# A gated recurrence with a max of three products: another order of all engines' work in the first three steps

## The chip, the cores and the metric

The kernel runs on one core of a Trainium2 chip. The metric is device microseconds of one execution. Executions of one kernel mostly lie within one to two per cent of each other; a run is called slow when it is over 1.5% above the fastest of its kernel, and only fast runs are compared. Where a ratio stands below, it is the mean time of one kernel's fast runs over the mean of the kernel before's fast runs of the same rounds, with a 95% interval, so it is not quite the ratio of the medians that stand beside it. "Faster" and "slower" are said from 2% on.

## The reference, cut to what matters

```python
def _attn_ref(q, k, v, alpha):                 # 4 batches, 8 heads, 768 tokens, 48 wide
    for t in range(S):
        state = alpha[:, :, t, :, None] * state + einsum('bhd,bhe->bhde', k[:, :, t], v[:, :, t])
        y[:, :, t] = einsum('bhd,bhde->bhe', q[:, :, t], state)

def _moe_ref(x, w1, w2, w3, w_out):            # x 3072 x 384, w1..w3 384 x 768, w_out 768 x 384
    h = np.maximum(np.maximum(x @ w1, x @ w2), x @ w3)
    return h @ w_out
```

The output of the first, heads side by side, is x of the second. Inputs and output are float32; the kernel computes in fp16 with float32 sums.

## The kernel before

The tokens are cut into 12 steps of 256 (three chunks of each of four batches). In a step VectorE, GpSimd and ScalarE make scaled forms of q and k; TensorE transposes them (in the later steps the DMA engines do), multiplies them to scores (A), applies the masked scores to the values (Y, attend), updates the state (S), then runs nine groups of gate matmuls (G) with maxima behind them, and two projections (O). The whole program is one list of named pieces per engine order. A piece is a letter, a number, an optional engine or bank letter, and the step after "@".

```python
    pieces = {
        "l": load_step, "K": lambda _, i, *x: load_weight(i), "W": cast_weight, "H": warm,
        "m": pair_decay, "N": logs, "r": inverse, "u": near_k, "w": near_q,
        "c": sums, "e": decay_in, "f": decay_out, "g": totals,
        "k": scale_k, "q": scale_q, "V": values,
        "T": turn, "t": keep_turned, "D": turn_by_dma, "A": scores, "a": masked,
        "Y": attend, "x": keep_x, "M": gates, "S": update, "s": add_state, "z": decay_state,
        "G": gate, "h": maxed, "O": project, "o": store,
    }
    # ...
    with tc.manual_schedule():
        nc.vector.memset(blank, 0.0)
        clear_padding()
        emit(0, PROLOGUE)                      # steps 0, 1, 2 and the start of 3 and 4
        for s in range(3, NS):
            emit(s, LAST if s == NS - 1 else STEADY)
```

Each engine works through its own pieces in the order in which the list names them. A scaled product has two inputs in SBUF and may be given to VectorE ("v") or GpSimd ("p"):

```python
    def scaled(eng, s, r, i, n):
        dst = qks[s % NQ][:, r, i]
        engines[eng or "p"].tensor_mul(
            dst.rearrange("p a b c -> p (a b) c")[:, :, :D],
            near_of.pop((s, n)) if r == 0 else raw(n, s, 1), dec_of[s, n])
```

A gate group is twelve instructions of TensorE, six weight loads and six matmuls of 256 columns:

```python
        for j in range(2):
            jj = 2 * jg + j
            for f in range(NF):                # NF = 3
                nc.tensor.matmul(gps[:, j, :], wcat[:, f, g, jj * P:(jj + 1) * P],
                                 xT[:, f].rearrange("p u t -> p (u t)"),
                                 start=(f == 0), stop=(f == NF - 1))
```

Warm-up: matmuls of 512 columns on zeros whose result nobody reads (53 in the profiled run of the kernel before, 14.9 us busy).

```python
    def warm(_, n, *x):
        wps = bank([P, 512], "wps", "g")
        for _ in range(n):
            nc.tensor.matmul(wps, blank[:, :P], blank, start=True, stop=True)
```

## Time and profile before

| | kernel before |
|---|---|
| time, median of the 3 runs | 157.74 us (156.53 to 159.45) |
| span of the profiled run | 155.9 us |
| first gate matmul | 26.16 us |
| score matmuls of step 4 | 62.08 us |
| distance from one steady step to the next | 10.66 us |
| TensorE at half clock | 19.46 to 22.87 us, and after the end |

TensorE is busy everywhere but at the start, in the fifth slice (15.6 to 19.5 us), and at the end.

### The profile page before, as it was taken

The numbers are of one execution on the slowest core, as the hardware profiler recorded it, in microseconds if no ns is written. First come the engines' busy times: TensorE is split into PE (matmuls) and PEld (weight loads), VectorE is DVE, ScalarE is ACT, GpSimd is POOL, SyncE is SP. The second block draws the span as 40 slices with busy tenths as digits, with TensorE's granted clock in tenths as the row PEclk, the third lists the DMA queues.
The fourth block names the chain that finished last, engine by engine and source line by source line (L and its number), as shares of the span: only waits on it lengthen the run. The fifth ranks groups of instructions, "written<-read, shape, count | busy, mean of one in ns | idle before, by whom it ended". The sixth has DMA issues, their size and how long they took to land.

```text
span 155.9 us, 5905 instructions
## 1 busy us (share of the span) xinstructions
PE 147.8 (95%) x2537; PEld 110.3 (71%) x2537; DVE 127.8 (82%) x210; ACT 77.3 (50%) x152; POOL 88.4 (57%) x128
## 2 busy tenths in 40 slices
PE   6999399999999989999999999999999999999990
PEld 2446177788787778687787786886877877868860
DVE  2239989999876998979989989989898898996560
ACT  3449359475778569165274362471643622023311
POOL 5146970932567908857967967687679674020000
PEclk9999959999999999999999999999999999999999
DMA  5999999999999997099999996989914909411013
GB/s 125 322 325 325 369 349 340 291 298 326 265 280 281 310 289 219 9 166 270 244 162 293 190 231 193 254 225 328 214 50 62 178 4 104 136 50 55 4 70 132
DMA packets 72889, 32.49 MB, mean 208 GB/s; under 512 B 65440, under 2 KB 72864, under 8 KB 72864
## 3 DMA queue, kind: packets, MB, share of 16 engines
q1 hardware_dynamic: 72576, 31.99, 82.6%
q8 instruction: 20, 0.33, 0.9%
q10 hardware_dynamic: 288, 0.13, 0.5%
q14 instruction: 5, 0.04, 0.1%
HBM read 23.73 MB, written 4.72 MB: 182 GB/s over the span
## 4 chain that ended last, share of the span: by engine, by line
PE 84%; DVE 6%; SPq 3%; DMA 3%; issue 1%; ACT 0%; DVEq 0%; ACTq 0%
PE gps L396 46%; PE ops L420 16%; PE yps L330 5%; PE aps L280 5%; PE yps L311 4%; PE sps L368 3%; SPq L95 3%; DMA ra<-in_alpha_dram 3%; PE tps L259 3%; DVE qk L235 1%; PE lps L209 1%; DVE vt L158 1%; PE wps L433 1%; DVE ka L199 1%; DVE pa L184 1%
## 5 line engine op out<-in xcount | busy, mean ns | idle before, releaser
L396 PE MATMUL gps<-xT,wcat 128*128 128x256 f16 x648 | 76.9, 273 | 0.7 <-DVE hT L411 0.7
L396 PEld LDWEIGHTS <-wcat 128*128 128x128 f16 x648 | 61.6, 98 | 10.0 <-issue 0.7
L287 DVE TENSOR_TENSOR lat<-aps,cp 128x512 f16<-128x512 f32 x48 | 30.1, 677 | 0.7 <-PE aps L280 0.7
L383 POOL TENSOR_TENSOR st<-full,gm 128x384 f16<-128x384 f32 x19 | 15.9, 839 | 21.4 <-DVE full L379 13.9
L411 DVE TENSOR_TENSOR h<-gps,h 128x512 f16<-128x512 f32 x36 | 24.4, 683 | 3.5 <-PE gps L396 1.6
L411 DVE TENSOR_TENSOR hT<-gps,h 128x512 f16<-128x512 f32 x36 | 24.5, 689 | 3.2 <-PE gps L396 0.9
L420 PE MATMUL ops<-wo,hT 128*128 128x384 f16 x144 | 27.1, 327 | 0.0
L156 ACT ACTIVATE ob<-ops,c 128x384 f32<-128x384 f32 x23 | 13.4, 583 | 18.7 <-PE ops L420 18.7
L420 PEld LDWEIGHTS <-hT 128*128 128x128 f16 x144 | 13.3, 98 | 7.5
L150 ACT CAST xT<-yps 128x384 f16<-128x384 f32 x14 | 6.5, 479 | 23.3 <-PE yps L330 23.3
L152 DVE CAST h<-gps 128x512 f16<-128x512 f32 x21 | 14.4, 690 | 2.1 <-PE gps L396 2.1
L150 ACT CAST h<-gps 128x512 f16<-128x512 f32 x15 | 8.8, 586 | 14.8 <-PE gps L396 14.7
L433 PE MATMUL wps<-blank 128*128 128x512 f16 x53 | 14.9, 435 | 1.2 <-DVE blank L506 1.2
L203 POOL TENSOR_TENSOR qa<-rq,ra 128x384 f32<-128x384 f32 x10 | 10.0, 1001 | 7.0 <-DMA rq<-in_q_dram 4.5
L353 POOL TENSOR_TENSOR gt<-ge 128x4 f32<-128x4 f32 x18 | 4.0, 220 | 13.9 <-ACT ge L229 13.9
L235 POOL TENSOR_TENSOR qk<-ka,ic 128x384 f16<-128x384 f32 x10 | 10.3, 1028 | 1.6 <-ACT ic L217 1.6
L199 POOL TENSOR_TENSOR ka<-rk,ra 128x384 f32<-128x384 f32 x10 | 10.3, 1033 | 1.4 <-DVE qk L235 1.4
L433 PEld LDWEIGHTS <-blank 128*128 128x128 f16 x53 | 5.4, 110 | 7.9 <-issue 3.3
L330 PE MATMUL yps<-lat,vt 64*32 64x128 f16 x768 | 10.9, 220 | 0.0
L235 POOL TENSOR_TENSOR qk<-qa,ac 128x384 f16<-128x384 f32 x9 | 9.1, 1010 | 2.1 <-ACT ac L223 2.0
L156 ACT ACTIVATE vt<-rv,c 128x768 f16<-128x768 f32 x11 | 10.2, 930 | 0.0
L150 ACT COPY qkT<-tps 128x1024 f16<-128x1024 f16 x7 | 7.0, 1009 | 5.3 <-PE tps L259 5.2
(53 smaller groups left out, 181.1 us busy)
## 6 DMA issues: line engine op xcount, KB each, us to landing
ra<-in_alpha_dram SPq DMA_DIRECT2D x12, 384.0 KB, 5.2
rk<-in_k_dram SPq DMA_DIRECT2D x12, 384.0 KB, 5.3
rq<-in_q_dram SPq DMA_DIRECT2D x12, 384.0 KB, 5.1
rv<-in_v_dram SPq DMA_DIRECT2D x12, 384.0 KB, 5.0
out_dram<-ob SPq DMA_DIRECT2D x24, 192.0 KB, 3.4
ws<-in_moe_w_dram SPq DMA_DIRECT2D x9, 384.0 KB, 7.0
ws<-in_moe_w_out_dram SPq DMA_DIRECT2D x3, 384.0 KB, 6.3
qkT<-qk SPq DMA_TRANSPOSE x14, 4.5
```

What stands on the lines that cost most here:

```text
L150: nc.scalar.copy(out=dst, in_=src)
L152: engines[eng].tensor_copy(out=dst, in_=src)
L156: nc.scalar.mul(dst, src, col)
L199: engines[eng or "p"].tensor_mul(near_of[s, "k"], raw("k", s, 0), raw("a", s, 1))
L235: engines[eng or "p"].tensor_mul(dst.rearrange("p a b c -> p (a b) c")[:, :, :D], near_of.pop((s, n)) if r == 0 else raw(n, s, 1), dec_of[ ...
L287: nc.vector.tensor_mul(lat_of[s, u][:, i].rearrange("p (a r) t -> p a r t", r=R), aps_of[s, u][i].rearrange("p (a r) t -> p a r t", r=R), ...
L330: nc.tensor.matmul(yps[x][C * m:C * (m + 1), f, :], vt[rows, r * HP + p].rearrange("p a b -> p (a b)")[:, at:at + C], lats[p // (HP // R)] ...
L383: engines[eng or "p"].tensor_mul(sts[s % B][1 - x].rearrange("p a (b d) -> p a b d", d=D), full_of.pop((s, x)), gm_of.pop((s, x)).unsqueez ...
L396: nc.tensor.matmul(gps[:, j, :], wcat[:, f, g, jj * P:(jj + 1) * P], xT[:, f].rearrange("p u t -> p (u t)"), start=(f == 0), stop=(f == NF ...
L411: nc.vector.tensor_max(h, gps, h_of[s, i - 1])
L420: nc.tensor.matmul(ops, hT_of[s][:, jj, u * P:(u + 1) * P], wo16[:, jj, :], start=(jj == 0), stop=(jj == NJ - 1))
L433: nc.tensor.matmul(wps, blank[:, :P], blank, start=True, stop=True)
```

## The change

The intent is to order the work of all engines in the first three steps afresh, so that fewer of VectorE's SBUF products run at the same time as GpSimd's. No arithmetic changes. The diff replaces the three strings of pieces; their first lines and one steady step:

```diff
     PROLOGUE = """
-        m0v@0 r0@0 r1@0 H2@0 H1@0 H4@0 H2@0 H2@0 H3@0 l0@1 w0p@0 u0v@0
-        H2@0 l0@2 l1@2 l1@1 N0@0 l2@1 c0@0 l2@2 l3@1 K4@0 H2@0 e0@0
-        H2@0 m0v@1 H1@0 N0@1 H2@0 H2@0 f0@0 m0v@2 H3@0 H4@0 r0@2 K3@0
-        g0@0 r0@1 V0v@0 N0@2 H3@0 k1p@0 K0@0 H1@0 H2@0 c0@1 e0@1 q1v@0
(4 lines cut)
-        A0g@0 a3@0 a0@0 a2@0 a1@0 l3@3 l1@4 l2@4 T1g@2 t0a@1 H3@0 l0@5
-        r1@2 H2@0 M0p@0 z0p@0 t1a@2 s1@0 w0v@2 l3@4 A1@1 a2@1 V0@1 W4p@0
-        Y0g@0 x0v@0 W3a@0 x1@0 W0p@0 W1a@0 q0v@2 M0p@1 A0g@1 S0@1 s0a@1 a0@1
-        z0p@1 W2a@0 W5p@0 a3@1 G0@0 l3@5 T0@2 G1@0 a1@1 G3@0 l1@5 W7p@0
-        W6a@0 h0v@0 G4@0 h3@0 G2@0 W8p@0 s1a@1 m0p@3 Y0@1 t0@2 x1@1 h1@0
+        r0@0 l0@1 H8@0 m0v@0 l0@2 r1@0 H3@0 N0@0 l1@1 H2@0 c0g@0 H1@0
+        l2@1 w0v@0 e0@0 k1p@0 f0@0 l3@1 l2@2 l1@2 q0p@0 g0@0 H3@0 H2@0
+        H1@0 l3@2 H2@0 q1v@0 H3@0 H3@0 l0@3 u0v@0 M0v@0 H2@0 k0v@0 m0v@2
+        l0@4 V0@0 T0@0 T1@0 t0@0 m0p@1 r0@1 K0@0 K1@0 r1@1 K3@0 K2@0
(4 lines cut)
+        T1g@1 T0g@1 H2@0 V0@1 q0v@2 t1a@1 t0@1 u0v@2 S0@1 A0g@1 V0@2 k1p@2
+        s0a@1 l1@5 M0v@1 A1@1 a0@1 q1p@2 Y0g@0 r0@3 l1@4 a2@1 k0p@2 T1g@2
+        a1@1 x0@0 l0@5 t1a@2 l3@6 l2@6 z0p@1 a3@1 T0@2 Y0g@1 t0@2 x1@0
+        A1g@2 A0@2 m0p@3 m0p@4 s1@1 x0@1 l3@4 W0v@0 a2@2 l2@5 x1@1 M0v@2
+        W1a@0 N0@4 S0@2 W3p@0 W2p@0 G0@0 s0@2 a3@2 W5p@0 G0@1 a1@2 W4p@0
(the rest of both PROLOGUEs cut)
     STEADY = """
-        T0@1 G0@0 N0@2 t0a@1 c0@2 g0@2 f0@2 G3@0 u0p@2 T1@1 G4@0 h0v@0
-        e0@2 M1p@-2 z1p@-2 h3v@0 G5@0 r0@3 r1@3 h4@0 G1@0 G6@0 h5@0 h1@0
-        t1a@1 M0p@1 k0p@2 S0@1 k1v@2 w0p@2 V0@2 s0@1 z0p@1 A0g@1 q1p@2 D1@2
+        w0v@2 T1g@1 N0@2 t1@1 M0p@1 u0p@2 T0@1 G0@0 G3@0 h3@0 c0@2 G4@0
+        g0@2 e0@2 t0a@1 h0v@0 G5@0 G1@0 V0@2 f0@2 h4@0 h5@0 h1@0 M1p@-2
+        k0v@2 z1p@-2 G6@0 S0@1 A0g@1 k1p@2 s0@1 h6@0 A1@1 O1g@-1 O0@-1 z0p@1
(the rest of STEADY, and LAST, cut)
```

In the old order the first gate (G0@0) stands between the attends of steps 0 and 1 (Y0g@0, Y0@1). In the new one both attends, the remaining transposes and the scores of step 2 come before it.

More of the change, by code (lines that the diff above doesn't have):

```diff
@@ L463 @@
     PROLOGUE = """
-        m0v@0 r0@0 r1@0 H2@0 H1@0 H4@0 H2@0 H2@0 H3@0 l0@1 w0p@0 u0v@0
-        H2@0 l0@2 l1@2 l1@1 N0@0 l2@1 c0@0 l2@2 l3@1 K4@0 H2@0 e0@0
-        H2@0 m0v@1 H1@0 N0@1 H2@0 H2@0 f0@0 m0v@2 H3@0 H4@0 r0@2 K3@0
-        g0@0 r0@1 V0v@0 N0@2 H3@0 k1p@0 K0@0 H1@0 H2@0 c0@1 e0@1 q1v@0
-        H2@0 K1@0 k0v@0 K2@0 K6@0 K5@0 r1@1 l3@2 c0g@2 H2@0 K7@0 S0@0
-        g0@2 k1v@1 K8@0 u0v@2 M0v@2 q0p@0 l0@3 w0v@1 l0@4 g0@1 l2@3 f0@1
-        T0@0 e0@2 q1v@1 T1@0 K11@0 f0@2 k0v@2 q0v@1 t0a@0 H3@0 H3@0 u0p@1
@@ L471 @@
-        l1@3 t1a@0 T1g@1 s0a@0 K9@0 K10@0 A1@0 k1p@2 k0p@1 t1@1 T0g@1 q1p@2
-        A0g@0 a3@0 a0@0 a2@0 a1@0 l3@3 l1@4 l2@4 T1g@2 t0a@1 H3@0 l0@5
-        r1@2 H2@0 M0p@0 z0p@0 t1a@2 s1@0 w0v@2 l3@4 A1@1 a2@1 V0@1 W4p@0
-        Y0g@0 x0v@0 W3a@0 x1@0 W0p@0 W1a@0 q0v@2 M0p@1 A0g@1 S0@1 s0a@1 a0@1
-        z0p@1 W2a@0 W5p@0 a3@1 G0@0 l3@5 T0@2 G1@0 a1@1 G3@0 l1@5 W7p@0
-        W6a@0 h0v@0 G4@0 h3@0 G2@0 W8p@0 s1a@1 m0p@3 Y0@1 t0@2 x1@1 h1@0
-        h4@0 h2@0 A0g@2 a0@2 x0@1 a1@2 A1@2 G6@0 h6v@0 V0@2 G5@0 h5@0
@@ L478 @@
-        S0@2 s0a@2 l0@6 r0@3 l1@6 m0p@4 G0@1 h0v@1 a2@2 G1@1 l3@6 r1@3
-        N0@3 G7@0 G3@1 l2@6 h1@1 h7@0 G8@0 G6@1 l2@5 h3@1 h6@1 h8@0
-        a3@2 G2@1 z0v@2 c0@3 h2@1 g0@3 r0@4 w0p@3 G4@1 Y0g@2 N0@4 G7@1
-        f0@3 M0p@3 x1@2 u0p@3 x0@2 h4@1 q0v@3 q1v@3 G5@1 e0@3 G0@2 h7@1
-        G8@1 c0@4 h5@1 r1@4 h0@2 G6@2 G1@2 k0p@3 G7@2 h8@1 h6v@2 k1p@3
-        W10a@0 l2@7 G8@2 W11a@0 g0@4 V0@3 h7@2 h1@2 T0g@3 W9p@0 O1@0 T1@3
-        M1v@0 h8@2 f0@4 s1a@2 o1@0 O0g@1 t1a@3 t0@3 u0p@4 e0@4 z1p@0 o0@1
@@ L485 @@
-        G3@2 S0@3 A0g@3 h3@2 l1@7 l0@7 l3@7 s0@3 a1@3 w0p@4 a0@3 q1v@4
-        q0p@4 A1@3 z0p@3 r0@5 O0g@0 a2@3 G2@2 O1@1 a3@3 o0@0 m0v@5 r1@5
-        V0@4 G4@2 Y0g@3 h2@2 k1p@4 h4@2 x0v@3 o1@1 G5@2 h5@2 s1@3 x1@3
-        k0p@4
+        r0@0 l0@1 H8@0 m0v@0 l0@2 r1@0 H3@0 N0@0 l1@1 H2@0 c0g@0 H1@0
+        l2@1 w0v@0 e0@0 k1p@0 f0@0 l3@1 l2@2 l1@2 q0p@0 g0@0 H3@0 H2@0
+        H1@0 l3@2 H2@0 q1v@0 H3@0 H3@0 l0@3 u0v@0 M0v@0 H2@0 k0v@0 m0v@2
+        l0@4 V0@0 T0@0 T1@0 t0@0 m0p@1 r0@1 K0@0 K1@0 r1@1 K3@0 K2@0
@@ new lines @@
+        K5@0 S0@0 K4@0 K6@0 K7@0 K8@0 s0a@0 l1@3 t1@0 H2@0 u0p@1 r0@2
+        l2@3 r1@2 H1@0 A0g@0 A1g@0 N0@1 K9@0 H2@0 K11@0 a2@0 z0p@0 K10@0
+        a0@0 c0@1 e0@1 w0p@1 a1@0 H4@0 g0@1 k0v@1 l2@4 N0@2 a3@0 k1p@1
+        f0@1 c0@2 s1a@0 f0@2 e0@2 q1v@1 l3@3 H3@0 g0@2 w0p@2 H2@0 q0v@1
+        T1g@1 T0g@1 H2@0 V0@1 q0v@2 t1a@1 t0@1 u0v@2 S0@1 A0g@1 V0@2 k1p@2
+        s0a@1 l1@5 M0v@1 A1@1 a0@1 q1p@2 Y0g@0 r0@3 l1@4 a2@1 k0p@2 T1g@2
+        a1@1 x0@0 l0@5 t1a@2 l3@6 l2@6 z0p@1 a3@1 T0@2 Y0g@1 t0@2 x1@0
@@ new lines @@
+        A1g@2 A0@2 m0p@3 m0p@4 s1@1 x0@1 l3@4 W0v@0 a2@2 l2@5 x1@1 M0v@2
+        W1a@0 N0@4 S0@2 W3p@0 W2p@0 G0@0 s0@2 a3@2 W5p@0 G0@1 a1@2 W4p@0
+        W6p@0 h0@0 N0@3 a0@2 G1@1 z0v@2 G1@0 r0@4 h0@1 G3@0 s1a@2 r1@4
+        c0@3 G2@0 Y0@2 h1@1 h1@0 x0@2 h2@0 G2@1 h3v@0 G4@0 h2@1 c0@4
+        G5@0 f0@3 h4@0 G6@1 W7a@0 h5@0 G6@0 r1@3 e0@3 x1v@2 G7@0 W8p@0
+        h6v@0 g0@3 G3@1 M0v@3 h6@1 g0@4 G8@0 G7@1 h7@0 h8@0 G4@1 u0v@3
+        w0p@3 h3@1 G5@1 h7@1 e0@4 G8@1 G0@2 M1p@0 q1v@3 f0@4 z1p@0 W9a@0
@@ L489 @@
+        k0p@3 h4@1 h5@1 h8@1 k1v@3 l1@6 l3@5 G6@2 G8@2 G7@2 h6@2 h7@2
+        h8@2 T1@3 l0@6 q1v@4 h0@2 w0v@4 G3@2 h3@2 G4@2 q0p@3 W10p@0 t1@3
+        T0g@3 W11p@0 O1g@0 O0g@0 V0@3 S0@3 t0@3 h4@2 s0a@3 o1v@0 A1@3 l0@7
+        z0p@3 o0@0 A0g@3 O0g@1 a3@3 a0@3 a1@3 O1@1 G5@2 a2@3 o1v@1 h5@2
+        Y0g@3 m0p@5 r0@5 l1@7 l3@7 o0@1 s1@3 G1@2 r1@5 x1@3 x0@3 G2@2
+        q0p@4 u0p@4 k1p@4 V0@4 k0v@4 l2@7 h1@2 h2@2
     """
     STEADY = """
-        T0@1 G0@0 N0@2 t0a@1 c0@2 g0@2 f0@2 G3@0 u0p@2 T1@1 G4@0 h0v@0
@@ L492 @@
-        e0@2 M1p@-2 z1p@-2 h3v@0 G5@0 r0@3 r1@3 h4@0 G1@0 G6@0 h5@0 h1@0
-        t1a@1 M0p@1 k0p@2 S0@1 k1v@2 w0p@2 V0@2 s0@1 z0p@1 A0g@1 q1p@2 D1@2
-        A1@1 h6@0 a1@1 O0g@-1 G7@0 a0@1 O1@-1 a2@1 a3@1 q0p@2 D0@2 Y0g@1
-        o0@-1 h7@0 s1@1 G8@0 l3@5 x0@1 m0p@3 G2@0 o1@-1 x1v@1 h8@0 h2@0
-        l2@5 l0@5 l1@5
+        w0v@2 T1g@1 N0@2 t1@1 M0p@1 u0p@2 T0@1 G0@0 G3@0 h3@0 c0@2 G4@0
+        g0@2 e0@2 t0a@1 h0v@0 G5@0 G1@0 V0@2 f0@2 h4@0 h5@0 h1@0 M1p@-2
+        k0v@2 z1p@-2 G6@0 S0@1 A0g@1 k1p@2 s0@1 h6@0 A1@1 O1g@-1 O0@-1 z0p@1
@@ L497 @@
+        G7@0 a0@1 a2@1 q0p@2 q1p@2 a1@1 a3@1 D0@2 D1@2 Y0g@1 s1@1 m0v@3
+        h7@0 o1@-1 o0@-1 x0@1 G8@0 x1v@1 h8@0 G2@0 h2@0 l1@5 l3@5 l2@5
+        l0@5 r0@3 r1@3
     """
     LAST = """
-        G0@0 G3@0 G1@0 G2@0 h0v@0 G7@0 h1@0 h2@0 h3@0 G6@0 h6@0 O1@-1
-        G8@0 G4@0 h7@0 h8@0 h4@0 G5@0 o1@-1 O0g@-1 h5@0 O1@0 O0@0 o0@-1
+        G0@0 G7@0 G6@0 h6v@0 O0@-1 G3@0 h0@0 G8@0 h7@0 h3v@0 G1@0 h8@0
+        h1@0 G4@0 G5@0 o0@-1 h4@0 h5@0 G2@0 h2@0 O1g@-1 o1@-1 O1@0 O0@0
         o1v@0 o0@0
```

## The prediction

> **Names.** A piece is a letter, a number and the step after "@": c sums, T transposes, A scores, Y attend, S state update, G one of a step's nine gate groups, O output projection, H n warm-up matmuls of no use, W0 to W11 casts of weights. A last letter v, p or a puts the work on VectorE, GpSimd or ScalarE.
>
> **What bounds the kernel now.** I read the page's first two parts, then the chain that ended last, then the timelines of TensorE, VectorE and GpSimd one after another. From the chain:
>
> ```profile
> 62.08 0.57 PE aps L280 x32
> ...
> 72.75 0.57 PE aps L280 x32
> ...
> 83.42 0.57 PE aps L280 x32
> ...
> 94.08 0.57 PE aps L280 x32
> ```
>
> The columns are start, duration and what. The score matmuls of a steady step return every 10.66 us, and TensorE is busy between them: one step is A 0.57, two O 0.98 + 1.08, Y 1.33, nine G at 0.655 (5.9), S 0.44 and c about 0.3, together 10.6. So steady steps are TensorE's own work; a new order there can lose time, not gain it. VectorE is next: 18.7 us busy in the four stretches from 85 to 105 us, 94%. The only idle times of TensorE over 0.5 us after the first gate are one of 0.67 us ("DVE hT", at 55.7) and small ones of 0.2 to 0.3. What can be won lies before the first gate, and TensorE's timeline shows it:
>
> ```profile
> 7.18 4.91 PE L433 MATMUL wps<-blank 128*128 128x512 f16 x22
> ...
> 14.12 1.07 PE L259 MATMUL tps<-cp,qk 128*128 128x128 f16 x16
> 15.03 1.46 PE L433 MATMUL wps<-blank 128*128 128x512 f16 x6
> 18.89 0.62 PE L259 MATMUL tps<-cp,qk 128*128 128x128 f16 x8 [2.41 <-DVE qk L235]
> ...
> 26.16 0.81 PE L396 MATMUL gps<-xT,wcat 128*128 128x256 f16 x6
> ```
>
> L433 is warm-up, so from 7.2 to 18.9 us TensorE does some 3 us of useful work. At 18.89 it has waited 2.41 us for a product of VectorE; the first gate is at 26.16. The two engines behind that wait, VectorE first:
>
> ```profile
> 13.92 1.35 DVE L199 TENSOR_TENSOR ka<-rk,ra 128x384 f32<-128x384 f32 x1
> 15.19 0.95 DVE L353 TENSOR_TENSOR gt<-ge 128x4 f32<-128x4 f32 x1
> 16.18 0.92 DVE L355 TENSOR_TENSOR gm<-gt,c 128x8 f32<-128x8 f32 x1
> 17.02 0.55 DVE L203 TENSOR_TENSOR qa<-rq,ra 128x384 f32<-128x384 f32 x1
> 17.49 1.34 DVE L235 TENSOR_TENSOR qk<-rq,ac 128x384 f16<-128x384 f32 x1
> ```
>
> ```profile
> 13.61 1.24 POOL L199 TENSOR_TENSOR ka<-rk,ra 128x384 f32<-128x384 f32 x1 [1.43 <-DVE qk L235]
> 14.81 1.31 POOL L235 TENSOR_TENSOR qk<-rk,ic 128x384 f16<-128x384 f32 x1
> 16.09 0.99 POOL L235 TENSOR_TENSOR qk<-ka,ic 128x384 f16<-128x384 f32 x1
> 17.04 1.38 POOL L235 TENSOR_TENSOR qk<-rq,ac 128x384 f16<-128x384 f32 x1
> ```
>
> A VectorE product takes 0.55 us undisturbed (17.02) and 1.35 beside GpSimd; the 4-element gt takes 0.95 where the same operation at 46.6 us took 0.15. They alternate: the VectorE product of 13.92 ends at 15.27, some 0.45 after GpSimd's ended at 14.85, and GpSimd's next, from 14.81, ends 0.85 after that. [...]
>
> [...] 48 masks have a mean of 0.677 us, close to their 0.68 with GpSimd idle. [...] here warm-up matmuls are issued every 0.43 us until 5.4 us, then every 0.21. So 13 of them before c@0 rather than 16 end about 0.5 us earlier.
>
> **The change part by part.** The arithmetic stays: the same pieces, of which some 60 move between VectorE, ScalarE and GpSimd. Although it is named for the first steps, the diff also rewrites the steady and last orders.
>
> *Before the first gate.* Before it, the old order does T@0, T@1, T1@2, A@0, A@1, Y@0, S@0, S@1; the new one also T0@2 (0.45), A@2 (0.57), Y@1 (1.17, from 29.97 to 31.14) and S@2 (0.45). TensorE's total is fixed (warm-ups: 53 to 46), so what counts is the first gate's start less this: break-even is 26.16 + 2.64 = 28.80 us.
>
> *When the new first gate can start.* Its W0 is now VectorE's, after nearly all of two steps' work there. I walk the queues with the measured durations.
> - c@0 at 6.3; its two exponentials end at 7.3 and 7.6. VectorE then has q1, u, M and k0 of step 0 (0.47 each back to back, M 0.3) beside GpSimd's k1, q0 and m@1. Free of collisions, T0@0 starts at 10.0; strictly alternating, at 12.0. It was 14.12.
> - The two transposes (0.9), two copies on VectorE (1.2) and A (0.6 with its latency): masks begin between 12.5 and 15.2, against 20.3.
> - From there to the end of W0 VectorE needs: eight masks 4.8, four products for q and k of steps 1 and 2 1.9, t0@1 and t0@2 1.2, u@2 0.47, M 0.3, s1 twice 1.0, W0 0.5 to 0.8: 10.3 us. Waiting for T0@1 and A@1 adds about 0.6; collisions with GpSimd's k1@1, w@2, k1@2, q1@2, k0@2 add 0 to 2.9.
> - End of W0: best 12.5 + 10.3 + 0.6 = 23.4; worst 15.2 + 10.3 + 0.6 + 2.9 = 29.0. The best is cut by two things. The first weight now comes after 14 loads of steps, not 11; at 1.2 us each and 5 to 7 us to landing it arrives at 22 to 24, and the following, cast by GpSimd, every 1.0 to 1.2 us. ScalarE begins step 1's logarithm only after s0@0, so c@1, at 11.93 before, moves to 13.5 to 15.6. I take 25.3 to 29.0.
>
> The walk's worst case is pessimistic where it lets the engines alternate each time; the intent says that collisions become fewer. I choose 27.2: a gain of 28.8 - 27.2 = 1.6 us.
>
> *From the first gate to step 3.* Old: 26.16 to 62.08, 35.9 us, of which 34.5 is useful work by my addition (27 + 6 gates 21.6, four O 3.9, and 9.0 of T, A, Y, S and c). At most 1.4 can be won. VectorE starts this stretch with eight pieces of step 2 (4.3 us) ahead of its first maximum, but four gate banks and ScalarE's copies cover that. I count 0 for that.
>
> *Steady steps.* VectorE gains w (0.47) and m (0.47) and loses a copy to ScalarE (0.67); its k product, 0.95 now because it collides, may fall to 0.55. From 10.0 of 10.66 it comes to 9.9, or to 11.2 if all three collide at 0.95. TensorE waits only if m, now ahead of the maximum of gate 7, is late: after the last mask come s1 0.5, m 0.5 to 0.9 and the maximum 0.6, 1.6 to 2.0 in all, and the bank is wanted 2.0 after the mask. I allow 0.1 us for each of six steps as a mean of 0 and 0.2: plus 0.5, rounded down as I think 0 likelier. GpSimd falls from about 8.5 to 6.5 us a step, worth nothing.
>
> *End.* Nine gates and four projections remain in both last orders, 5.9 + 3.9 us; 0 within 0.2.
>
> Sum: 157.74 - 1.6 + 0.3 = 156.4; of the 1.4 us of stalls between the first gate and step 3 a better order should find a third, which makes 156.0.
>
> **Rivals.**
> 1. [...] VectorE's products now stand at T0@0 and T0@1 beside GpSimd's own, and more queue ahead of W0 than before. For it: strict alternation in the trace. Against: masks and copies from PSUM lie between them. First gate at 29: 157.9, no change.
> 2. *The collisions go and the weights' landing becomes the bound.* First gate at 25.3, gain 3.5: 154.2. For it: the transfers run at some 325 GB/s without a gap from 5 us on. It needs both engines' queues free of waits.
> 3. *VectorE becomes the steady bound.* It is at 94%; if all its SBUF products collide, a step needs 11.2 us of it and seven steps lose up to 0.5 each: 159 to 160. Against: GpSimd is idle for 4 us of each new step.
>
> **Range and chances.** 2% is 3.15 us, so faster needs nearly all of rival 2, and slower needs rivals 1 and 3 together with more. The three runs of before spread over 2.9 us. I take 153.0 to 158.6, with 0.25 faster, 0.70 within 2%, 0.05 slower.
>
> **What would show it.** Right: T0@0 near 11, first gate near 27 with three S and three A ahead of it, score matmuls of steady steps 10.66 us apart, those at 62.08 now near 60.4, VectorE's k product at 0.55 in steady steps. Wrong: a first gate at 29 with VectorE's products at 0.9 to 1.35 (rival 1), or at 25 (rival 2); a period above 10.7 with "DVE h" waits of TensorE (rival 3); or gates after the first that wait for weights or for VectorE's backlog of step 2.

## More of the kernel before

Attend is 64 small matmuls on tiles of 64 by 32 (and 12 on the state in the first four steps, 24 later), each with a weight load of its own (the page of the changed kernel counts 768 matmuls and 768 loads of this line in 12 steps), so over 150 instructions:

```python
                        nc.tensor.matmul(
                            yps[x][C * m:C * (m + 1), f, :],
                            vt[rows, r * HP + p].rearrange("p a b -> p (a b)")[:, at:at + C],
                            lats[p // (HP // R)][rows, i, p % (HP // R) * R + r, :], ...)
```

From the page of the kernel before: busy time of each engine with its share of the span, then TensorE's busy share and the granted clock in 40 equal slices (9 is 90% or more, 5 is half speed), then the queue that carries instructions (transfers, MB, share).

```profile
PE 147.8 (95%) x2537; PEld 110.3 (71%) x2537; DVE 127.8 (82%) x210; ACT 77.3 (50%) x152; POOL 88.4 (57%) x128
...
PE   6999399999999989999999999999999999999990
...
PEclk9999959999999999999999999999999999999999
...
q8 instruction: 20, 0.33, 0.9%
```

## The result

| | before | changed |
|---|---|---|
| median | 157.13 us (156.47 to 159.45, 4 runs) | 162.65 us (161.96 to 163.71, 4 runs) |
| span of the profiled run | 155.9 us | 160.1 us |
| ratio | | 1.0371 [1.027, 1.0473]: slower |

The four runs of the changed kernel are fast. Of the four of the kernel before, 159.45 us is slow by the rule of 1.5%, and the ratio leaves it out. The time lies 4 us above the predicted range. The page of the changed kernel:

```profile
PE 147.5 (92%) x2530; PEld 109.7 (69%) x2530; DVE 131.8 (82%) x222; ACT 77.2 (48%) x154; POOL 79.9 (50%) x114
...
PE   7978678399999999999999999999999999999990
...
PEclk9999999779999999999999999999999999999999
...
q8 instruction: 20, 0.33, 0.8%
...
L330 PE MATMUL yps<-lat,vt 64*32 64x128 f16 x768 | 11.3, 221 | 2.8 <-issue 2.8
```

GpSimd has indeed lost work (88.4 to 79.9 us). But the eighth slice of TensorE, 28 to 32 us, is only 30% busy, and the clock is reduced there. The last line is attend's group; its final column says that TensorE stood idle for 2.8 us ahead of one of these matmuls, and that nothing in the profile released it: "issue". TensorE's timeline (start, duration, what, count, idle before) shows the place:

```profile
27.51 0.29 PE L330 MATMUL yps<-lat,vt 64*32 64x128 f16 x10
30.57 0.30 PE L330 MATMUL yps<-lat,vt 64*32 64x128 f16 x6 [2.77 <-issue]
30.80 1.07 PE L280 MATMUL aps<-qkT 48*64 48x128 f16 x32
31.80 0.82 PE L368 MATMUL sps<-vt,qk 64*128 64x96 f16 x16
32.55 4.03 PE L396 MATMUL gps<-xT,wcat 128*128 128x256 f16 x30
```

The attend of step 1 stops after 10 of its last 16 matmuls. These 16 use the same values and the same masked scores as the ones before them; no data can be missing for six of them alone. Then all that follows is stretched: the scores take 1.00 us from start to start where they took 0.57, the first gate matmuls 0.21 us each instead of 0.11. The same kinds of work in the kernel before:

```profile
27.26 2.78 PE L396 MATMUL gps<-xT,wcat 128*128 128x256 f16 x24
...
31.14 0.64 PE L280 MATMUL aps<-qkT 48*64 48x128 f16 x32
```

The view of one stretch says why (columns: stretch, its length, busy time of TensorE, weight load, VectorE, ScalarE and GpSimd with counts, granted clock, DMA share, GB/s):

```profile
30.36:33.77 3.41, 3.20 (x60) 2.44 (x60) 2.05 (x6) 2.02 (x4) 1.67 (x3) 0.50 1.07 295
```

The clock is granted at half speed (0.50) for 3.41 us, from 30.36, 0.21 us before TensorE runs again after 2.77 us of idle time.

**Where the 4.2 us of span went.** The standstill is 2.77. The half clock costs 0.43 on the scores (1.00 against 0.57, by starts), 0.30 on the state update (0.75 against 0.45) and 0.58 on the first 30 gate matmuls (3.86 against 3.28 in h1 and c1 below), together 1.31. The sum is 4.08. It is all there by step 4, and little is added after it. From the chain that ended last:

```profile
66.16 0.57 PE aps L280 x32
...
76.83 0.57 PE aps L280 x32
```

Step 4 begins 4.08 us later than before (62.08), and the steady distance is 10.67.

**The kernel before has a half clock too.** Its profiled run has one such stretch (19.46 to 22.87), the changed one has one. The mean granted clock of a run tells how many it had: one stretch of 3.41 us in 156 makes 0.989. Of 39 runs of the kernel before in the rounds of s1, s2, h1 and r1, the five at 0.998 or more took 156.6 to 157.0 us, the 28 at 0.987 to 0.989 took 157.6 to 158.9, the five at 0.978 took 159.0 to 159.3. So one stretch costs it about 1.2 us (an estimate from these runs), and the sum above is not the whole comparison: the half clocks of the two kernels nearly cancel, and beside the standstill some 1.3 us (4.2 - 2.77, less the 0.1 by which 1.31 exceeds 1.2) must come from the new start itself. The experiments h1 and c1 show from where.

**What stopped TensorE.** What I found at the standstill is a transfer of the instruction queue. It makes 20 transfers of 16,384 bytes in either kernel. I counted TensorE's records (matmuls and weight loads each count one). From the start of the first transfer to that of the last TensorE begins 4,829 records in the kernel before (190 to 5,019) and 4,796 in the changed one (221 to 5,017), 254 and 252 from one transfer to the next. In this kernel and in the experiments below, the standstills without a data wait came after record 701, 702, 703 or, in c1, 957, so 254 to 256 apart. From these counts I estimate that TensorE gets its instructions in blocks of about 256, one transfer (a fetch, below) for each, and that a new block begins at about record 191 + 256k; the exact record is an inference, and so is that the transfers are TensorE's. The times in the tables are read from the records and the packets of the trace, as no view prints them. As the fetch of the block from 703 on I take the transfer that starts next after record 447, where by this count the block before it is entered:

| run | enters 447 at | fetch of the next block | enters 703 at | gap there |
|---|---|---|---|---|
| before | 24.70 | 27.36 to 28.43 | 30.33 | none |
| changed | 24.05 | 27.84 to 28.92 | 30.57 | 2.99 |

The gap is from one matmul's start to the next one's, so it is 0.2 us more than the idle time in the timeline. In both kernels the fetch starts 2.7 to 3.8 us after the block was entered and takes 1.1. Resumption follows its end by 1.65. The kernel before needed its new block 1.90 us after the fetch had ended, and so passed with a quarter of a microsecond to spare, if it takes as long to resume. It got through because it spends 5.6 us on the 256 instructions from 447 to 703: 30 gate matmuls of 0.11 us are among them, 24 of them in the line shown above. The changed kernel runs a whole series of small matmuls there, attend, transposes, attend, and was through in 3.5 us. This is theory F (fetch), an inference that the experiments below test. The rival C says that collisions between VectorE and GpSimd, or something else that the new order does to data, delays TensorE (some expectations below call it D or V).

### The profile page after: what moved, and what is told of

It is laid out like the page before. It is cut to its first block, busy times and chain, and to the rows that moved or that the text cites.

```text
span 160.1 us, 5903 instructions
## 1 busy us (share of the span) xinstructions
PE 147.5 (92%) x2530; PEld 109.7 (69%) x2530; DVE 131.8 (82%) x222; ACT 77.2 (48%) x154; POOL 79.9 (50%) x114
## 4 chain that ended last, share of the span: by engine, by line
PE 85%; DVE 8%; issue 4%; ACT 1%; ACTq 0%; DVEq 0%
PE gps L396 44%; PE ops L420 15%; PE yps L330 6%; PE wps L433 4%; PE aps L280 4%; PE yps L311 4%; PE sps L368 3%; PE tps L259 3%; DVE qk L235 3%; DVE ka L199 1%; PE lps L209 1%; DVE lat L287 1%; DVE h L411 1%; DVE gm L355 1%; ACT ic L217 1%
## 5 line engine op out<-in xcount | busy, mean ns | idle before, releaser
L420 PE MATMUL ops<-wo,hT 128*128 128x384 f16 x144 | 25.5, 327 | 0.0
L150 ACT CAST h<-gps 128x512 f16<-128x512 f32 x24 | 14.0, 586 | 23.3 <-PE gps L396 20.6
L156 ACT ACTIVATE ob<-ops,c 128x384 f32<-128x384 f32 x21 | 12.2, 581 | 22.9 <-PE ops L420 22.9
L353 POOL TENSOR_TENSOR gt<-ge 128x4 f32<-128x4 f32 x16 | 5.8, 362 | 19.4 <-ACT ge L229 19.4
L433 PE MATMUL wps<-blank 128*128 128x512 f16 x46 | 13.7, 447 | 2.0 <-DVE blank L505 1.2
L235 POOL TENSOR_TENSOR qk<-rk,ic 128x384 f16<-128x384 f32 x11 | 11.0, 996 | 6.1 <-ACT ic L217 5.0
L330 PEld LDWEIGHTS <-vt 64*32 64x32 f16 x768 | 7.4, 90 | 5.4 <-issue 2.9
L235 POOL TENSOR_TENSOR qk<-qa,ac 128x384 f16<-128x384 f32 x10 | 10.6, 1059 | 0.0
L152 DVE CAST h<-gps 128x512 f16<-128x512 f32 x12 | 8.2, 686 | 1.6 <-PE gps L396 1.6
L259 PE MATMUL tps<-cp,qk 128*128 128x128 f16 x80 | 6.0, 219 | 3.7 <-DVE qk L235 3.4
```

Of the source, the lines that this page charges most:

```text
L150: nc.scalar.copy(out=dst, in_=src)
L156: nc.scalar.mul(dst, src, col)
L235: engines[eng or "p"].tensor_mul(dst.rearrange("p a b c -> p (a b) c")[:, :, :D], near_of.pop((s, n)) if r == 0 else raw(n, s, 1), dec_of[ ...
L259: nc.tensor.transpose(tps[:, i, p, :], qks[s % NQ][:, r, i, p].rearrange("p a b -> p (a b)"), ident)
L330: nc.tensor.matmul(yps[x][C * m:C * (m + 1), f, :], vt[rows, r * HP + p].rearrange("p a b -> p (a b)")[:, at:at + C], lats[p // (HP // R)] ...
L420: nc.tensor.matmul(ops, hT_of[s][:, jj, u * P:(u + 1) * P], wo16[:, jj, :], start=(jj == 0), stop=(jj == NJ - 1))
```

## The experiments

All outputs are right.

### Which string holds the loss

```diff
 s1:  PROLOGUE of the changed kernel
-     STEADY, LAST of the changed kernel
+     STEADY, LAST of the kernel before
```

> The new order of the first three steps with the old steady and last orders. Theory F: TensorE's standstill of 2.8 us inside the attend of step 1 is a wait for its next block of 256 instructions, asked for while the transfers of weights are queued; with the half clock that follows it is nearly the whole loss. So this run keeps it: ratio to before 1.03 to 1.04, a gap of 2 to 3 us at TensorE's instruction 703, first gate at 32 to 33. Rival S, the rewritten steady and last orders cost part of it: ratio below 1.02.

163.41 us median (4 runs), ratio 1.0336 [1.0266, 1.0407].

```diff
 s2:  STEADY, LAST of the changed kernel
-     PROLOGUE of the changed kernel
+     PROLOGUE of the kernel before
```

> The old order of the first three steps with the new steady and last orders. Theory F: no gap, ratio 0.995 to 1.005. Rival S: ratio above 1.015.

157.53 us median (20 runs) against 157.82, ratio 0.9971 [0.9945, 0.9997]. The whole loss is in the first steps; the new steady order even gains 0.3%. That is what the steady VectorE shows. A scaled product of k, first in the kernel before, then in the changed one:

```profile
83.19 0.95 DVE L235 TENSOR_TENSOR qk<-rk,ic 128x384 f16<-128x384 f32 x1
```

```profile
87.18 0.55 DVE L235 TENSOR_TENSOR qk<-ka,ic 128x384 f16<-128x384 f32 x1
90.97 0.55 DVE L184 TENSOR_TENSOR pa<-ra 128x384 f32<-128x384 f32 x1
```

The first (0.95 us) began 0.53 us before the end of a GpSimd product (82.72 to 83.72), the second (0.55) 0.12 us before the end of one (86.30 to 87.30). So the k product no longer collides, and neither does the pair product that VectorE took over (0.55). VectorE's busy time in a steady distance falls from 10.01 to 9.80 us, GpSimd's from 8.17 to 6.65.

### An earlier fetch by quiet data queues

TensorE's fetch takes place while the loads of data run (340 GB/s from 24 to 28 us in the kernel before, 362 in the changed one). Here the loads from the third weight on wait on GpSimd until the time of the fetch, so that the data queues are nearly empty (each load named in the last two lines is taken from its old place):

```diff
+    def hold(_, i, *x):
+        nc.gpsimd.memset(stage[i][:, :1], 0.0)      # piece Q; the load into stage[3] waits for it
 PROLOGUE of the changed kernel:
-    ... K0@0 K1@0 r1@1 K3@0 K2@0 K5@0 S0@0 K4@0 K6@0 K7@0 K8@0 s0a@0 l1@3 t1@0 ...
+    ... K0@0 K1@0 r1@1 S0@0 s0a@0 t1@0 ...
-    ... a2@1 k0p@2 T1g@2 ...
+    ... a2@1 k0p@2 Q3@0 K3@0 K2@0 K5@0 K4@0 K6@0 K7@0 K8@0 l1@3 l2@3 K9@0 K11@0 K10@0
+        l2@4 l3@3 l1@5 l1@4 T1g@2 ...
```

> The changed kernel, with the third weight transfer and all later loads held until GpSimd has finished its product for k of step 2 (a memset of one column of that weight's buffer stands there, so that the transfer has to wait for it, at about 24.7 us). The transfer queues are then nearly empty when TensorE enters its third block of instructions at 24.0 us. Theory F: the fetch starts within 1.2 us of that in place of 3.8, the gap at instruction 703 falls from 3.0 to under 0.6 us, no half clock at 30 us, first gate at 29 to 29.6 (VectorE's cast of the first weight ends at 28.9), ratio 1.00 to 1.015 although the weights land up to 6 us later. Rival D, the gap is a wait for data or buffers: gap unchanged, ratio 1.035 or more.

158.8 us median over 20 runs, ratio 1.0021 [0.999, 1.0051]. This kernel scatters: about 8 of its 20 runs, from 159.4 us up, count as slow and are left out, and only one run was traced, so it is open whether the long ones had a standstill (one of them, 160.18 us, had a mean clock of 1.0, so no half clock made it long). If they had, the hold does not always help, and the ratio of the fast runs holds for the cases where it does; the mean of all 20 is 159.4 us (157.9 before). The traced one (158.51 us, fast) had nearly none. TensorE's timeline at the same place:

```profile
28.13 0.29 PE L330 MATMUL yps<-lat,vt 64*32 64x128 f16 x10
28.60 0.24 PE L330 MATMUL yps<-lat,vt 64*32 64x128 f16 x6 [0.19 <-issue]
...
29.79 3.45 PE L396 MATMUL gps<-xT,wcat 128*128 128x256 f16 x30
```

The stop is after the same ten matmuls, but 0.19 us long. The stretch from 24 to 28 us of the changed kernel, then of this one (columns as above):

```profile
24.00:28.00 4.00, 3.45 (x158) 2.50 (x143) 4.00 (x8) 2.00 (x4) 3.83 (x5) 1.00 1.11 362
```

```profile
24.00:28.00 4.00, 4.00 (x198) 3.15 (x192) 3.96 (x8) 2.76 (x5) 3.67 (x5) 1.00 0.32 96
```

With 96 GB/s of data instead of 362, and none at all from 23.3 us until the fetch, the fetch started 0.83 us after its block was entered (25.16), not 3.79, and ended at 27.25; record 703 was entered at 28.60, 1.35 later. Except for the loads and the hold, order, engines and products are those of the changed kernel. Theory F holds for the standstill. Without it the new order is no slower than the old one in the mean, but its fast runs were at full clock more often: 8 of 12 had a mean clock of 0.996 or more, against 6 of 34 of the kernel before. At like clock h1 is slower: 157.1 to 158.9 us at 0.996 or more (156.6 to 157.7 before), and 158.5 to 159.1 at 0.984 to 0.989 (157.6 to 158.9, median 157.8, before). About 1 us is thus left that is not the standstill.

### Fewer small matmuls before the boundary

```diff
-    ... T0@2 Y0g@1 t0@2 x1@0 A1g@2 A0@2 m0p@3 m0p@4 s1@1 x0@1 l3@4 W0v@0 a2@2 l2@5 x1@1 M0v@2 ...
+    ... T0@2 t0@2 x1@0 A1g@2 A0@2 m0p@3 m0p@4 s1@1 l3@4 W0v@0 a2@2 l2@5 M0v@2 ...
-    ... W2p@0 G0@0 s0@2 ...
+    ... W2p@0 G0@0 Y0g@1 x0@1 x1@1 s0@2 ...
```

> The changed kernel with the attend of step 1 (and its two evictions) moved behind the first gate, so that the scores of step 2, the state update and the first gate come before it. The same instructions; fewer of them stand in a row before the first gate, which waits for VectorE's cast anyway. Theory F: instruction 703 is reached at about 30 us in place of 27.6, the gap there is under 1 us, first gate at 29 to 29.5, ratio 1.00 to 1.02. Rival D: the gap inside the attend stays at 2.5 us or more, ratio 1.03 or more.

161.13 us (4 runs), ratio 1.0214 [1.0163, 1.0265]: some two fifths of the loss are back, slightly less than I had expected. Its timeline:

```profile
31.38 0.50 PE L330 MATMUL yps<-lat,vt 64*32 64x128 f16 x36 [0.35 <-issue]
...
33.32 0.93 PE L396 MATMUL gps<-xT,wcat 128*128 128x256 f16 x7 [0.98 <-ACT xT L150]
```

The stop shrinks from 2.77 to 0.35 us and the clock stays full, as F has it, for now 6.5 us lie between entering the two blocks (24.88 and 31.38). What I had not reckoned with are data waits that the removed attend used to cover: 1.19 us before the scores of step 2 (at 28.48), and 0.98 us of the gate of step 1, whose x is now late.

### Are the collisions enough?

Kernel c1 is h1 with all of step 0's products on VectorE, without any of GpSimd's beside them; c2 is the same with the loads left where the changed kernel has them.

```diff
-    ... H8@0 m0v@0 l0@2 ... w0v@0 e0@0 k1p@0 f0@0 ... q0p@0 g0@0 ... q1v@0 ... u0v@0 M0v@0 H2@0 k0v@0 ...
+    ... H8@0 m0v@0 u0v@0 l0@2 ... e0@0 f0@0 ... g0@0 w0v@0 k1v@0 k0v@0 q1v@0 q0v@0 M0p@0 ...
```

> The changed kernel with the held loads (as h1_quiet), and with all six products of step 0 on VectorE, in an order that uses its idle time (k0 times alpha before q0 lands), step 0's two gate products on GpSimd: no product of step 0 can collide. Prices the collisions of step 0. If they are on the path to the first gate (rival 1 of the prediction): transposes of step 0 finish by 10.5 us (12.7 in the changed kernel), first gate 1.5 to 2.3 us earlier than h1_quiet's 29.8, ratio 0.985 to 0.995. If the later chain (ScalarE's exponentials, landings) decides: first gate within 0.6 us of h1_quiet's, ratio 1.00.

c1: 156.69 us (12 runs), ratio 0.9953 [0.9917, 0.9989], on the edge of what I expected. The transposes of step 0 run in one piece at 10.19 us, where the changed kernel interrupts them by 0.98 us of waiting and begins the second part at 11.89. The first gate starts at 27.50, 2.3 earlier than in h1 (a part of this is a half clock that h1 has from 20.48 to 23.89 and c1 has not). All 12 runs have a mean clock of 0.995 or more; in the same rounds the kernel before took 156.5 to 156.9 us at 0.997 or more. So c1 wins back the 1 us that h1 had lost, and beats the kernel before only in that none of its runs shows a half-clock stretch. The stop moved to the next boundary (after record 957) and is short:

```profile
33.09 0.35 PE L330 MATMUL yps<-lat,vt 64*32 64x128 f16 x20 [0.36 <-issue]
```

> c1_no_collision without the held loads: the changed kernel with step 0's products on VectorE alone. Separates what c1 won by fewer collisions from what it won by quiet queues. Theory F: weights are queued when TensorE asks for its fourth block, so a gap of 1 to 3.5 us at instruction 703 returns, first gate 29 to 31, ratio 1.01 to 1.03. If the collisions alone had been the fault of the changed kernel (rival V): no gap, ratio 0.99 to 1.00 as in c1.

c2: 161.19 us (4 runs), ratio 1.0223 [1.0168, 1.0277]. Its timeline:

```profile
25.90 0.28 PE L330 MATMUL yps<-lat,vt 64*32 64x128 f16 x9
28.58 0.31 PE L330 MATMUL yps<-lat,vt 64*32 64x128 f16 x7 [2.40 <-issue]
```

With the collisions of step 0 gone TensorE arrives at the boundary 1.6 us sooner and stands still there for 2.40 us, again with the half clock after it (28.18 to 35.01). So the collisions of step 0 are not what stops TensorE. They cost those 1.6 us: c1 shows that removing them gains (0.9953 against h1's 1.0021), but only if the instructions come.

### The loss made in the kernel before

If F is right, small matmuls put into the kernel before must bring the standstill there too, although nothing of its data changes.

```diff
+    def crowd(_, n, *x):
+        wps = bank([P, 512], "wps", "g")
+        for _ in range(n):
+            nc.tensor.matmul(wps, blank[:, :P], blank, start=True, stop=True)
+        for i in range(48):                             # 96 in p2
+            m, rows = i % 4, slice(0, J)
+            nc.tensor.matmul(wps[C * m:C * (m + 1), :P],
+                             blank[rows, :C], blank[rows, :P], start=True, stop=True)
 p1, PROLOGUE of the kernel before:
-    ... T1g@2 t0a@1 H3@0 l0@5 ...
+    ... T1g@2 t0a@1 P3@0 l0@5 ...
 p2, PROLOGUE of the kernel before:
-    ... Y0g@0 x0v@0 W3a@0 x1@0 W0p@0 W1a@0 q0v@2 M0p@1 A0g@1 ...
+    ... Y0g@0 x0v@0 W3a@0 x1@0 W0p@0 W1a@0 q0v@2 M0p@1 P0@0 A0g@1 ...
```

> The kernel before, with 48 small matmuls of the attend's shape (no use, into the bank of a warm-up) added to that warm-up at 22.4 us, where TensorE is ahead anyway. Alone they cost about 1 us, partly in a wait. Theory F: they make 96 more instructions, so TensorE enters its next block that much earlier in its work, at about 28.5 us in place of 30.3, while the block lands no earlier than before (the fetch ended at 28.4 and TensorE needs 1.5 us more). So a gap of 1 to 2 us with no releaser appears at instruction 703, among the gates; ratio 1.008 to 1.025. Rival D: no such gap, ratio 1.00 to 1.006.

p1: 158.66 us (17 runs), ratio 1.0057 [1.0027, 1.0087], and no standstill in the traced run. My expectation missed. Its blocks explain how, though not why: the block was entered at 23.93, the fetch ran from 24.92 to 26.04, only 0.99 us later with the loads of the kernel before, where 351 GB/s ran during a lag of 2.66 us, and record 703 was entered at 28.02. The added matmuls ran at 22.26 and moved the boundaries as planned: the block lasted 4.09 us, 5.63 before. What spared it was the early fetch. So the lag between entry and fetch does not seem to be set by the traffic of data alone.

> The kernel before, with 96 small matmuls of the attend's shape (192 instructions, no use) between the attend of step 0 and the scores of step 1, right behind the point at which TensorE enters its third block of instructions (24.7 us in before). In p1_crowd 48 of them took 0.8 us, so these take 1.6 to 2.2. Theory F: the next block is needed 192 instructions earlier in the work, at about 27.5 us, and cannot be there before about 29 (in all runs TensorE entered a block no sooner than 1.3 us after its fetch had ended): a gap of 1 to 3 us with no releaser at instruction 703, which none of the data explains; ratio 1.015 to 1.04. Rival D: no gap beside the added work, ratio 1.008 to 1.015.

p2 puts twice as many into the block itself. 164.63 us (4 runs), ratio 1.0413 [1.0324, 1.0502]. Its timeline:

```profile
25.47 1.52 PE L441 MATMUL wps<-blank 64*32 64x128 f16 x96
26.92 0.30 PE L280 MATMUL aps<-qkT 48*64 48x128 f16 x7
29.92 0.52 PE L280 MATMUL aps<-qkT 48*64 48x128 f16 x9 [2.69 <-issue]
```

1.52 us of work that nobody needs cost 6.3 us (164.63 against 158.31 in the same rounds). TensorE stops within the scores, after record 702, for 2.69 us, and the half clock follows (29.68 to 33.09). The order of all other work, and its collisions, are those of the kernel before. The standstill is therefore made by small instructions in a row, where the fetch comes late, and not by the new order as such.

### A version that beats both

The last question is whether an early start can be had together with gates between the small matmuls. Kernel i1 brings step 0's attention forward, with its products on VectorE as in c1, and loads the first weight before the values of step 1, so that the gates of step 0 can stand between the attends; from step 2 on it takes the order of the kernel before, with the new steady order.

```diff
-    m0v@0 r0@0 r1@0 H2@0 H1@0 H4@0 ... (the first half of PROLOGUE before)
+    m0v@0 r0@0 r1@0 H8@0 H3@0 H2@0 l0@1 l0@2 u0v@0 N0@0 l1@1 l2@1 c0@0 e0@0
+    f0@0 g0@0 K0@0 l3@1 w0v@0 V0@0 l1@2 l2@2 H6@0 k1v@0 k0v@0 q1v@0 q0v@0
+    ... g0@2 V0@1 W0a@0 Y0g@0 K6@0 K5@0 K7@0 K8@0 k0v@1 q1v@1 q0v@1 T1g@1 x0@0
+    x1@0 s1@0 G0@0 T0g@1 ... S0@1 A0g@1 A1@1 ... W3p@0 G1@0 Y0g@1 ...
```

> An attempt to beat both: step 0's products on VectorE as in c1, both steps' exponentials before ScalarE's other work, the first weight loaded before the values of step 1, gates of step 0 between the attention of steps 1 and 2, then the old order of the rest with the new steady and last orders. Theory F: gates spread between the attends keep TensorE from outrunning its instructions, so the gap at 703 is under 1 us. First gate near 17 us with the attend of step 0 behind it; at 26 us some 5 us more useful work done than before. Ratio 0.96 to 0.985; above 0.99 if weights' landing or VectorE holds it.

156.03 us (8 runs), ratio 0.9932 [0.9889, 0.9975], far from the 0.96 to 0.985 that I expected. The first gate starts at 18.15. Two mended forms followed; i1 once more.

```diff
 i2, i1 with:
-    ... K3@0 K4@0 K2@0 ... V0@1 W0a@0 Y0g@0 ... k0p@2 q1p@2 z0p@1 ...
+    ... K2@0 K3@0 K4@0 ... (W0 on GpSimd, z0@1 ahead of the products of step 2, four gates of step 0 ahead of the scores of step 2, and moves around them)
 i3, i1 with:
-    ... u0p@1 z0p@0 k1p@1 w0p@1 e0@2 ... V0@1 W0a@0 Y0g@0 ... q0v@1 T1g@1 ... k0p@2 q1p@2 z0p@1
+    ... u0p@1 z0p@0 k1p@1 w0p@1 W0p@0 e0@2 ... V0@1 Y0g@0 ... q0v@1 H3@0 T1g@1 ... z0p@1 k0p@2 q1p@2
```

> i1_early mended where its profile shows waits: the state of step 1 decayed before GpSimd's products of step 2, the first weight cast on GpSimd, evictions of step 0 ahead of the values of step 1 on ScalarE, both transposes of step 1 before the first gate and copied by VectorE, four gates of step 0 between the attend of step 1 and the scores of step 2. If those waits were what i1 lost: attend of step 1 at 21 us (23.9 in i1), TensorE busy from 16 us on but for the gap at instruction 703, ratio 0.965 to 0.985. Theory F says that block 4 of instructions cannot be entered before about 25.5 us (26.5 in i1), so no more than 1.5 us beyond i1 can be won before the gates; ratio not below 0.975.

> i1_early once more, beside its mended form: ratio 0.988 to 0.997.

> i1_early with three edits: the state of step 1 decayed before GpSimd's last products of step 2, the first weight cast on GpSimd (idle there) in place of ScalarE, three more warm-up matmuls before the transposes of step 1. Expected: attend of step 1 0.8 to 1.1 us earlier than i1's 23.9, first gate 0.7 us earlier than 18.15; ratio 0.983 to 0.993 if the clock stays as in i1.

i2: 156.81 us (4 runs), ratio 0.9893 [0.9786, 1.0001], short of the 0.965 to 0.985 expected; its profiled run is slow. i1 again: 155.74 us (6 runs), ratio 0.9874 [0.9826, 0.9922]. i3: 156.46 us (22 runs), ratio 0.9929 [0.9904, 0.9954]; I had hoped that it would beat i1, and it does not, as TensorE still waits 1.74 us for a state that GpSimd computes (z0@1) before its attend at 23.49. So i1 beats both kernels, by about 1% of the kernel before over its 14 runs, under the 2% from which I say "faster". In the trace of its second submission it meets the boundary at record 703 inside the gates:

```profile
18.35 1.44 PE L396 MATMUL gps<-xT,wcat 128*128 128x256 f16 x6 [0.74 <-ACT xT L150]
...
27.53 1.70 PE L396 MATMUL gps<-xT,wcat 128*128 128x256 f16 x14 [0.52 <-issue]
```

It starts its gates 7.8 us before the kernel before does, and gains only 2 us, because it fills this time badly: the half clock lasts from 15.11 to 21.93, waits for data remain, and the boundary still costs 0.52 us.

### The fetches of the fast traces side by side

| run | enters 447 | fetch of next block | lag | enters 703 | after fetch | gap |
|---|---|---|---|---|---|---|
| before | 24.70 | 27.36 to 28.43 | 2.66 | 30.33 | 1.90 | none |
| changed | 24.05 | 27.84 to 28.92 | 3.79 | 30.57 | 1.65 | 2.99 |
| h1 | 25.16 | 25.99 to 27.25 | 0.83 | 28.60 | 1.35 | 0.40 |
| r1 | 24.88 | 28.72 to 29.88 | 3.84 | 31.38 | 1.50 | 0.56 |
| c1 | 22.54 | 23.46 to 24.49 | 0.92 | 26.09 | 1.60 | none |
| c2 | 22.42 | 26.04 to 27.18 | 3.62 | 28.58 | 1.40 | 2.61 |
| p1 | 23.93 | 24.92 to 26.04 | 0.99 | 28.02 | 1.98 | none |
| p2 | 24.97 | 27.46 to 28.60 | 2.49 | 29.92 | 1.32 | 2.90 |
| i1, first | 21.34 | 24.03 to 25.17 | 2.69 | 26.48 | 1.31 | none |
| i1 again | 21.53 | 24.93 to 26.01 | 3.40 | 27.53 | 1.52 | 0.79 |
| i3 | 20.06 | 22.25 to 23.18 | 2.19 | 27.62 | 4.44 | none |
| s2 | 25.01 | 27.18 to 28.11 | 2.17 | 30.64 | 2.53 | none |

No run entered the block sooner than 1.31 us after the end of its fetch (a record more or less is 0.1 us). Where the lag was not short (h1, c1, p1), it took 2.2 to 3.8, the transfer 0.9 to 1.2 and resuming 1.3 to 1.65: together, as an estimate, 4.4 to 6.6 us for which the 256 instructions of the block before must last. The lag is not the same in every run of one kernel: i1 came through without a stop at a lag of 2.69, and with one at 3.40.

## Why the prediction was wrong

**The step that failed.** "TensorE's total is fixed (warm-ups: 53 to 46), so what counts is the first gate's start less this." The total of work is fixed, but not the time that TensorE takes for it. The step had no term for the supply of its instructions, and none of the three rivals named it. The term measured 2.77 us of standstill, with 1.31 us of half clock after it; the growth of the span was 4.2. As the kernel before pays about 1.2 us for a half clock of its own, the standstill is the larger part of the difference, and the rest is the later start below. The standstill had its cause in what the same section lists, two attends, transposes and scores ahead of the first gate: taken as durations that add up to a break-even, they were right; as some 530 instructions that must be fetched (264 matmuls with a weight load each, by the counts of the timeline from 22.68 to 32.55 us), they were not looked at.

**The start of the first gate.** I chose 27.2 between 25.3 and 29.0. It came at 32.55; less 2.77 of standstill and 0.73 of half clock on scores and state update it is 29.05, estimated, the worst case of the walk, and h1 measured 29.79 with nearly no standstill, but with a half clock from 20.48 on. W0's cast ended at 28.93, the walk's own worst case of 29.0. So even without the standstill the gain of 1.6 us was wrong, and it was nil at best: h1's ratio is 1.0021. The reason is rival 1, the worst case that I had called pessimistic: c1, without collisions in step 0, has its first gate at 27.50, near the 27.2 that I chose, and c2 came 1.6 us sooner than the changed kernel to record 703. From the start of the changed kernel, VectorE and then GpSimd beside it:

```profile
8.94 1.35 DVE L199 TENSOR_TENSOR ka<-rk,ra 128x384 f32<-128x384 f32 x1
10.21 0.96 DVE L353 TENSOR_TENSOR gt<-ge 128x4 f32<-128x4 f32 x1
...
19.13 1.24 DVE L235 TENSOR_TENSOR qk<-rq,ac 128x384 f16<-128x384 f32 x1
```

```profile
8.56 1.31 POOL L235 TENSOR_TENSOR qk<-qa,ac 128x384 f16<-128x384 f32 x1
9.83 1.31 POOL L184 TENSOR_TENSOR pa<-ra 128x384 f32<-128x384 f32 x1
```

The two engines still alternate: the two operations of GpSimd end at 9.87 and 11.14 us, the first two of VectorE at 10.29 and 11.17, and VectorE's product takes 1.35 us where one at 11.28, with GpSimd idle, took 0.55. Before the first gate seven of VectorE's SBUF operations of two inputs ran at about 1.0 us or more, against four in the kernel before. The intent, fewer collisions, came true in the steady steps and not in the first ones; I took it from the words of the change instead of from the walk.

**From the first gate to step 3.** I counted 0. Measured from the first gate to the scores of step 4, it is 33.6 us (66.16 - 32.55). Before, the four pieces that the new order had already done (2.64) must be taken from 35.9, which leaves 33.3. The difference of 0.3 contains 0.58 of half clock on gates; without it the stretch would gain about 0.25, half of the "third of 1.4" that I had allowed.

**Steady steps and the end.** Right: the distance stayed at 10.67, VectorE fell to 9.80 (I had worked out 9.9), and the k product to 0.55. The 0.3 us of loss in my sum (0.5 in the paragraph before it, which does not agree) was not there; s2 measures a gain of 0.3% for the new steady and last orders. Rival 3 is refuted.

**Chances.** 0.05 for slower was too little, but no sum of the rivals named would have led to 1.037. A slip of the walk did not matter: 10.0 or 12.0 us plus 2.7 puts the first masks at 12.7 to 14.7, not at 12.5 to 15.2 (measured: 14.55). The three numbers that could have warned me were all in the profile before: 20 transfers of instructions, over 150 instructions in 1.2 us of attend against 12 in 0.655 us of a gate group, and a fetch that started 2.66 us after its block was entered.

**What stays open.** What sets the lag between the entry of a block and its fetch is not settled: it was 0.83 with no data under way (h1) and 0.92 where the data ran out just as the fetch began (c1: 373 GB/s at 22.5 us, 61 at 23.25, fetch at 23.46), 2.2 to 3.8 in the other traces (351 GB/s during the lag in the kernel before, 363 in the changed one), but 0.99 in p1, which has the loads of the kernel before. Nor is it settled what brings the half clock: it came with an idle time of 2.77 us in the changed kernel and of 2.41 us (before 18.89) in the kernel before, but not with the same 2.41 us (before 18.86) in p1. The stretch lasted 3.41 us (30.36 to 33.77 in the changed kernel), or twice that (28.18 to 35.01 in c2). Whether the long runs of h1 had standstills was not traced, and each kernel was traced once, i1 twice. The position of the boundaries is inferred from where the stops fell.

## What to carry to other kernels

When work is reordered, count instructions per microsecond as well as microseconds: in these traces, some 256 matmuls and weight loads that took less than about 4.5 to 6.5 us (the estimate below the table) could outrun the supply of instructions, and then cost a standstill of up to 2.77 us and, where it was 2.40 us or more (changed, c2, p2), a half clock after it. Keep long instructions between blocks of short ones; here gates between two attends did it, unnoticed. In a profile, idle time put down to "issue", in the middle of a group whose data is all there, was here the sign to look at the instruction queue's transfers (2.77 us, changed). And compare runs at like granted clock: here one half-clock stretch more or less moved a run by about 1.2 us, more than some of the differences in question.
